# A chunked linear-attention scan with a SoLU feed-forward: units batch by batch, whole-tensor loads, and DMA transposes from unit 12 on

## The chip, the cores and the metric

The kernel runs on one core of one Trainium2 chip. The metric is the device time in microseconds (us) of one execution. The core has TensorE (PE, its weight loads PEld), VectorE (DVE), ScalarE (ACT), GpSimd (POOL) and SyncE (SP). In this kernel SP issues every DMA, and 16 DMA engines move the bytes.

## The reference

Per batch and head a 48 x 48 state is decayed and fed token by token; the output of all heads goes through a feed-forward with SoLU and a norm.

```python
batch, n_heads, seq, head_dim = (4, 8, 768, 48)      # r, k, v, w: float32 of this shape; u: (8, 48)
n_tokens, d_model, d_ff = (3072, 384, 1024)
for t in range(S):
    cur = np.einsum('bhd,bhe->bhde', u[None] * kt, vt)
    y[:, :, t] = np.einsum('bhd,bhde->bhe', rt, state + cur)
    state = wt[:, :, :, None] * state + np.einsum('bhd,bhe->bhde', kt, vt)
...
x = y.transpose(0, 2, 1, 3).reshape(B * S, H * D)
h = x @ w_in
e = np.exp(h - h_max)
sm = e / (np.sum(e, axis=-1, keepdims=True) + 1e-09)
solu = h * sm
ln = (solu - mu) / np.sqrt(var + 1e-06) * g_ln
return (ln @ w_out).astype(np.float32)
```

## The kernel before

The sequence is cut into 6 chunks of 128 tokens. A unit is one chunk of one batch with all 8 heads, so there are 24 units. Before, unit i is chunk i // 4 of batch i % 4: the four batches go side by side, and a unit's state comes from the unit four earlier.

A unit goes through these steps. The names are the words of the order, the engine stands in brackets. LW, LK, LR, LV [SP] load w, k, r, v as float32, 192 KB each, in runs of 48 numbers. lw [ACT] takes the logarithm of w; cum [PE] sums it within the chunk; ex [ACT] takes the exponential; kp [DVE] scales k and r with it. krk and krr [PE] turn the scaled k and r (8 matmuls with an identity) into PSUM and kr [ACT or DVE] copies them out. M [PE] forms the scores, m [ACT or DVE] copies them, masked by sel [POOL] where ACT copied. p, q, qh [POOL] and dg [DVE] form the bonus of u, dv [POOL] multiplies it with v, which vb casts. Y [PE] forms the attention output (with the state if the chunk is not a batch's first), y [ACT or DVE] copies it. S [PE], et [ACT] and st [DVE] update the state. X [PE] turns y with 3 matmuls, and xT copies it.

The feed-forward: H [PE] multiplies with w_in, in 24 matmuls of 128 columns, so that the hidden numbers lie on the partitions and the tokens along the free side. e [ACT] is exp(h), he [DVE] is h times e, ea [POOL] adds halves of e for some units, hq [ACT or DVE] squares he. Oa and Ob [PE] multiply he with the centred, gained w_out (w2, 384 columns and one for the sum), and sum e (or ea) and hq with one-column matmuls into the same bank. sq [ACT], qm [DVE] and lv [ACT] (a logarithm and an exponential) give the norm's scale, o [ACT or DVE] applies it, out [SP] stores 192 KB.

The program is written out in one string, ORDER (lines 21 to 67). Each word names a step, a unit, and where there is a choice an engine or a PSUM bank. The class InOrder ties each instruction to the one before it on its engine, so every engine, SP's DMA issues too, works strictly in the sequence of the string. The weights are loaded, gained (gw), averaged (mn) and centred (ce) in the same string; hot are matmuls on zeros at the start. Nearly every instruction is recorded at line 86, the helper's, so the profile tells groups apart by tiles. Where a ring of buffers is short (NIO = 7 input buffers, NWK = 4, NKP = 6), a load or a write waits for the last reader.

Of the kernel before, what the change touches and what calls it, by code (L numbers as in the profile page):

```python
# [8 lines left out]
F32 = mybir.dt.float32  # L9
# [11 lines left out]
ORDER = """  # L21
LW2 LU0 ik0 lw2 hot5.4 cum2.0 LW1 lw1 us0.7 ih0 LW3 lw3 cum3.2 LR2 uc0 ex2 LK2 p2 LV2 vb2.p kp2 hot4.4 krk2.6 krr2
LR1 LK1 cum1.4 LW0 ex1 kp1 kr2.d hot1.0 S2.7 lw0 et2 LV1 vb1.d LW4 st2 p1 q1 hot2.0 krk1.1 krr1 q2 qh2 dg2 LG0
kr1.a M2.4 ex3 hot1.0 M1.6 m1.d dv2 LR0 LK0 p0 q0 cum0.0 ex0 lw4 cum4.6 ex4 kp0 krk0.1 krr0 LR3 gs0.0 gc0 dg1
m2.d Y2.i0 kr0.d LK3 p3 LR4 LV0 vb0.a dg0 dv1 kp3 Y1.i5 hot3.1 krk3.4 krr3 LK4 kp4 M0.2 m0.d krk4.1 y1.a X1.5
krr4 y2.a X2.0 dv0 xT2.d hot1.6 Y0.n7 y0.d kr3.a M3.2 hot1.0 X0.6 S1.4 p4 q3 kr4.a xT1.a xT0.a LI2 LI1 wi1.a
M4.0 m4.a et1 LI0 S0.5 et0 wi0.d m3.d LO1 wi2.p H1.6 e1 gw5.a H2.0 e2 H0.2 LO0 gw2.a q4 qh4 dg4 qh3 dg3 gw4.p
gw7.p LV3 vb3.p dv3 sel4 LW6 e0 gw6.d st1 LV4 vb4.p he1 lw6 dv4 gw1.d LW5 gw0.d gw3.d mn0.4 mc0 ce5.p ce6.p
Y3.i7 ce4.p he2 st0 he0 cum6.0 y3.a ce7.p hot1.5 X3.6 lw5 xT3.a ce3.d LK6 LR6 p6 Y4.n5 LR5 LK5 ce2.d hq0.a ex6
LW7 cum5.2 H3.6 p5 y4.d ex5 ce1.d ce0.d Oa0.5 kp6 krk6.1 krr6 S4.0 hq1.d Oa1.4 kp5 krk5.3 krr5 X4.2 Ob1 e3 he3  # L30
LV5 q6 q5 kr5.d hq2.a et4 st4 M5.6 kr6.a M6.0 xT4.d lw7 cum7.2 hq3.a sq1 m6.a m5.d dg5 vb5.d qm1 dv5 Ob0 ex7 sq0
qm0 S3.7 qh6 LR7 LK7 p7 kp7 et3 lv1 st3 lv0 H4.0 Y5.n6 y5.d LR9 LK8 o1.d e4 krk7.3 krr7 Oa2.2 he4 X5.7 q7 kr7.d
LW9 lw9 o0.a LK9 p9 LW8 lw8 S5.6 et5 cum9.4 ex9 Ob2 sq2 LR8 p8 st5 dg6 kp9 qm2 LV6 xT5.a LV9 vb6.p dv6 sel6
cum8.0 ex8 kp8 hq4.a LV7 LV11 out1 LW10 dg7 vb7.p dv7 Oa3.3 vb9.a lv2 H5.6 e5 M7.4 m7.d he5 q8 krk9.1 LK10 krr9
kr9.a S9.0 et9 Ob3 sq3 st9 q9 qm3 o2.a out0 ea5.p Y6.i5 y6.a LV8 LR10 Y7.n4 y7.d LW11 LW12 krk8.1 M9.6 lw10 lv3
X6.2 xT6.a m9.d o3.a krr8 LV10 out3 out2 kr8.d qh9 dg9 dg8 hq5.d cum10.4 ex10 kp10 S6.0 vb11.d et6 X7.2 xT7.a
st6 p10 vb8.d dv8 dv9 H6.6 e6 he6 H7.2 lw11 e7 he7 M8.4 m8.a Oa5.1 Y9.n0 Ob5 sq5 y9.d cum11.6 ex11 krk10.5 krr10
qm5 kr10.d S7.4 et7 st7 Oa4.3 hq6.d lv5 lw12 o5.a X9.2 sel8 Y8.i0 vb10.p y8.a LK11 LR11 kp11 xT9.d q10 dg10 p11
M10.4 m10.a sel10 S10.1 et10 st10 dv10 S8.0 et8 S11.7 et11 X8.6 xT8.a LK12 LW13 cum12.4 q11 ex12 lw13 st11 st8
Ob4 sq4 qm4 LW14 LR12 kp12 p12 lw14 lv4 o4.a out5 LK13 LV12 LR13 Y10.n2 dg11 y10.d H8.6 e8 krk12.1 krk11.0 krr11  # L40
krr12 kr12.d he8 kr11.a q12 qh12 cum13.4 H9.2 vb12.p S12.1 ex13 p13 q13 ea7.p dg12 kp13 dv11 LW16 LR14 LK14 e9
he9 et12 st12 M12.6 m12.a Oa6.0 X10.5 xT10.a krk13.4 krr13 kr13.a M11.6 m11.d ea8.p dv12 sel12 p14 cum14.2 ex14
q14 out4 Ob6 sq6 hq8.d M13.4 m13.d LV13 hq7.a LW15 lw15 lw16 kp14 vb13.d H10.6 dg13 qm6 LW18 lw18 Y11.n1 y11.d
Oa8.5 LK16 LR15 LR16 LK15 e10 he10 hq9.a krk14.4 Y12.i3 krr14 lv6 qh14 kr14.d p15 ea10.p dv13 LR18 LV14 vb14.p
q15 qh15 LK18 p18 Ob8 sq8 qm8 y12.a S13.2 et13 st13 o6.a lv8 X11.1 xT11.d cum16.6 ex16 X12.3 hq10.d LW19 kp16
Oa9.4 cum15.0 xT12.a Ob9 ex15 kp15 sq9 o8.a dg14 dv14 qm9 M14.2 m14.a sel14 krk16.7 Oa7.6 krr16 kr16.d lv9 o9.d
cum18.0 ex18 kp18 Ob7 LV15 S14.5 et14 st14 krk15.3 krr15 kr15.d LK19 Y13.i2 lw19 cum19.0 krk18.7 p16 q16 vb15.a
S15.4 y13.a sq7 qm7 dg15 X13.5 xT13.d ex19 LR19 kp19 lv7 o7.a q18 krr18 kr18.d H11.2 et15 st15 krk19.5 krr19
kr19.d LW17 lw17 cum17.0 e11 he11 ex17 ea11.p out8 LK17 LR17 p17 kp17 H12.6 e12 he12 hq11.a p19 H13.4 e13 Oa10.3
Y14.n2 M16.0 m16.a dg16 q19 dv15 y14.d ea12.p ea13.p M15.6 m15.d he13 Ob10 sq10 X14.2 out9 Oa11.1 LW20 qm10 lw20  # L50
cum20.6 hq12.d krk17.0 krr17 out6 out7 LV16 vb16.a dv16 xT14.a S16.2 LR20 ex20 LK20 dg18 et16 st16 lv10 o10.a
H14.4 e14 kp20 Ob11 sq11 kr17.d LK23 qm11 lv11 o11.a Oa12.2 krk20.3 krr20 kr20.a he14 sel16 Y16.n7 y16.d Y15.n6
y15.d M19.4 m19.a M18.0 m18.d Ob12 X15.7 xT15.a q17 hq13.d LV19 LW21 LV17 X16.3 xT16.a ea14.p vb19.a M17.4 m17.d
sq12 LK22 out10 qm12 dg17 qh19 vb17.p sel19 p20 hq14.a LW22 LV20 q20 qh20 dv17 M20.0 LV21 m20.d out11 LK21 H15.6
e15 he15 lw22 ea15.p H16.4 LV18 vb18.p dv18 LR21 p21 lw21 Oa14.3 Y17.n1 LR22 LV23 q21 dg19 dv19 Ob14 LR23 p23
p22 e16 he16 lv12 Oa13.0 LW23 o12.a out12 sq14 qm14 hq15.d vb20.a lv14 dg20 dv20 y17.d cum21.6 ex21 Ob13 cum22.4
sq13 ex22 LV22 vb22.p ea16.p o14.d out14 Y18.n2 y18.d Oa15.1 X18.3 qm13 kp22 lv13 xT18.d X17.2 xT17.a kp21 Ob15
sq15 qm15 S18.5 et18 st18 Y19.n4 y19.d lv15 o15.a out15 o13.a krk22.2 S17.3 et17 lw23 H18.6 e18 ea18.p hq16.d
vb21.d st17 Y20.n5 y20.d X19.4 xT19.d krr22 kr22.a H17.0 he18 hq18.d cum23.4 ex23 kp23 Oa16.3 e17 ea17.p he17
krk21.2 krr21 kr21.a H19.6 e19 krk23.5 X20.4 krr23 q22 qh21 vb23.p out13 xT20.a kr23.a he19 Oa18.2 Ob16 sq16  # L60
M21.0 q23 ea19.p qh23 dg22 dv22 m21.a sel21 qm16 lv16 M22.6 hq19.a M23.4 Ob18 sq18 dg21 H20.0 o16.a out16 m22.d
m23.d Oa19.7 Y22.n6 qm18 lv18 hq17.d Ob19 S19.5 dg23 dv23 e20 Oa17.4 y22.d X22.3 he20 et19 st19 xT22.d dv21
Y21.n6 Ob17 y21.d sq19 o18.a sq17 qm17 lv17 Y23.n1 out18 qm19 lv19 X21.0 xT21.d H22.2 o17.a e22 out17 ea20.p
y23.d H21.0 X23.5 xT23.a e21 hq20.d o19.d out19 Oa20.6 he22 hq22.d H23.4 e23 he21 hq21.d Ob20 sq20 qm20 lv20
o20.a out20 ea22.p Oa22.7 ea21.p Oa21.3 he23 hq23.d Ob22 sq22 qm22 lv22 Ob21 sq21 qm21 lv21 o21.d o22.a out22
out21 ea23.p Oa23.2 Ob23 sq23 qm23 lv23 o23.a out23
"""

NIO, NLW, NKP, NWK = 7, 10, 6, 4
# [24 lines left out]
def kernel(  # L94
# [22 lines left out]
    units = [(c, b) for c in range(NC) for b in range(B)]  # L117
# [30 lines left out]
    w_t = ring("w_in", NIO, [C, H, 64], F32)  # L148
    kr_t = ring("kr_in", NIO, [C, 2, H, 64], F32)
    v_t = ring("v_in", NIO, [C, H, 64], F32)  # L150
    win_f = consts.tile([128, KM, DF], F32)
    wout_f = consts.tile([128, KF, DM], F32)
    o_t = ring("o", NWK, [C, DM], F32)
# [28 lines left out]
    dve.memset(inv_col, 1.0 / RDF)  # L182
    ones_row = consts.tile([1, C], F32)
# [23 lines left out]
    st_t = [ring(f"st{b}_", 2, [C, H, D], BF16) for b in range(B)]  # L207
    xT_t = ring("xT", NWK, [128, KM, C], BF16)
    e_t = ring("e", NWK, [128, KF, C], BF16)
    ea_t = ring("ea", NWK, [128, KF // 2, C], BF16)  # L210
    he_t = ring("he", NWK, [128, KF, C], BF16)
    hq_t = ring("hq", NWK, [128, KF, C], BF16)
    sq_t = ring("sq", NWK, [C, 2], F32)
    qm_t = ring("qm", NWK, [C, 1], F32)
    lv_t = ring("lv", NWK, [C, 1], F32)
# [26 lines left out]
    def rows_of(src, i):  # L242
        c, b = units[i]
        return src[b, :, c * C:(c + 1) * C, :].rearrange("h t d -> t h d")

    def load_w(i, x):
        sp.dma_start(out=w_t[i % NIO][:, :, :D], in_=rows_of(w, i))

    def load_k(i, x):
        sp.dma_start(out=kr_t[i % NIO][:, 0, :, :D], in_=rows_of(k, i))  # L250

    def load_r(i, x):
        sp.dma_start(out=kr_t[i % NIO][:, 1, :, :D], in_=rows_of(r, i))

    def load_v(i, x):
        sp.dma_start(out=v_t[i % NIO][:, :, :D], in_=rows_of(v, i))
# [63 lines left out]
    def log_w(i, x):  # L320
        act.activation(out=lw_t[i % NLW][:, :, :D], in_=w_t[i % NIO][:, :, :D], func=LN)
# [11 lines left out]
    def scaled(i, x):  # L333
        ex = live[i]["ex"][:, :, :DM].rearrange("t a (h d) -> t a h d", h=H)
        dve.tensor_mul(out=kp_t[i % NKP][:, :, :, :D], in0=ex, in1=kr_t[i % NIO][:, :, :, :D])

    def bonus_rk(i, x):
        kr = kr_t[i % NIO]
        pool.tensor_mul(out=p_t[i % 3], in0=kr[:, 0, :, :D], in1=kr[:, 1, :, :D])
# [10 lines left out]
    def v_cast(i, x):  # L350
        copy = {"a": act.copy, "d": dve.tensor_copy, "p": pool.tensor_copy}[x]
        copy(out=vb_t[i % NLW], in_=v_t[i % NIO][:, :, :D])
# [49 lines left out]

    def attend(i, x):
        L = live[i]
        c, b = units[i]
        m, kr, vb = m_t[i % NWK], kr_s[i % NKP], vb_t[i % NLW]
        y_ps = L["y_ps"] = bank([C, DM], F32, x[-1], "y_ps")
        first = True
# [175 lines left out]
```

## Time and profile before

| what | value |
|---|---|
| median of 3 runs | 155.5 us (154.58 to 156.43) |
| span of the profiled execution, first to last instruction | 152.4 us |
| what the median has above that span | 3.1 us |
| mean granted TensorE clock | 0.975 |
| busy: PE, DVE, ACT, POOL | 136.4, 131.8, 120.0, 119.0 us |
| DMA moved | 27.06 MB in 104,825 packets, 100,314 of them under 512 bytes |
| a load of k, r or w: issue to landing | 3.7 us (median) |
| a store of a unit: issue to landing | 2.6 us (median) |

The profile is of one execution and gives it no other time than its span; the runs' times also hold what lies ahead of the first and behind the last instruction. Busy time is the union of a group's instructions; a matmul's end is modelled, so two matmuls in sequence overlap on paper, and their distance from start to start says what they cost. The slices are 40 equal parts of the span, a digit is a tenth of busy time.

### The profile page before, as it was taken

How to read it: one execution, taken by the hardware profiler on the slowest of the kernel's cores; microseconds unless marked ns; L12 is line 12 of the kernel's file. 1: busy time of each engine (PE TensorE's matmuls, PEld its weight loads, DVE VectorE, ACT ScalarE, POOL GpSimd, SP SyncE). 2: the span in 40 equal slices, each digit the busy share in tenths (PEclk: the TensorE clock that was granted, in tenths of full speed). 3: DMA queues.
4: the chain of work that ended last, by engine and by line, in shares of the span. 5: the costliest groups of instructions: out<-in, count | busy, mean ns of one | idle time of the engine just before them, and what ended most of it. 6: DMA issues, size and time to landing. Idle time of an engine off the chain costs nothing.

```text
span 152.4 us, 5172 instructions
## 1 busy us (share of the span) xinstructions
PE 136.4 (90%) x2093; PEld 105.5 (69%) x2093; DVE 131.8 (87%) x227; ACT 120.0 (79%) x247; POOL 119.0 (78%) x149
## 2 busy tenths in 40 slices
PE   6777598968999999999998999999799999999970
PEld 1242365936778889779776689887686988889740
DVE  5029968899999999998999999999999999988940
ACT  4526648869888999799998889998988789938661
POOL 7268986799909994899999997799889979973600
PEclk9959969999999999999999999999999999999998
DMA  3999999989979999989897989995998110112023
GB/s 76 218 216 211 217 334 377 254 175 223 216 151 216 220 204 229 206 177 224 194 203 144 228 195 275 199 199 136 241 205 210 63 45 4 44 63 103 4 79 127
DMA packets 104825, 27.06 MB, mean 178 GB/s; under 512 B 100314, under 2 KB 104419, under 8 KB 104803
## 3 DMA queue, kind: packets, MB, share of 16 engines
q1 hardware_dynamic: 104802, 26.75, 77.4%
q8 instruction: 16, 0.26, 0.7%
q14 instruction: 7, 0.05, 0.1%
HBM read 22.03 MB, written 4.72 MB: 176 GB/s over the span
## 4 chain that ended last, share of the span: by engine, by line
PE 53%; DVE 23%; SPq 8%; ACT 6%; issue 3%; DMA 2%; POOL 1%; DVEq 0%; POOLq 0%
PE ps L86 53%; SPq L86 7%; DVE he L86 6%; DVE m L86 4%; DVE kp L86 4%; DVE w L86 3%; DMA kr_in<-in_k_dram 2%; DVE kr L86 1%; DVE hq L86 1%; DVE y L86 1%; DVE st L86 1%; ACT ps L86 1%; ACT o L86 1%; DVE dg L86 1%; ACT win_sb L86 1%
## 5 line engine op out<-in xcount | busy, mean ns | idle before, releaser
L86 PE MATMUL ps<-w,he 128*128 128x385 bf16 x192 | 44.5, 325 | 1.0 <-DVE w L86 0.7
L86 PE MATMUL ps<-xT,win_sb 128*128 128x128 bf16 x576 | 35.5, 219 | 1.1 <-DVE qm L86 0.8
L86 PEld LDWEIGHTS <-win_sb 128*128 128x128 bf16 x576 | 32.8, 98 | 2.2 <-DVE m L86 0.9
L86 PE MATMUL ps<-one_col,hq 128*128 128x1 bf16 x192 | 31.5, 164 | 0.0
L86 DVE TENSOR_TENSOR he<-ps,e 128x1024 bf16<-128x1024 f32 x24 | 29.1, 1214 | 1.6 <-ACT e L86 1.6
L86 DVE TENSOR_TENSOR kp<-ps,kr_in 128x768 bf16<-128x768 f32 x24 | 22.8, 951 | 7.7 <-DMA kr_in<-in_k_dram 4.9
L86 POOL TENSOR_TENSOR p<-kr_in 128x384 bf16<-128x384 f32 x24 | 24.7, 1038 | 4.5 <-DMA kr_in<-in_k_dram 4.2
L86 POOL TENSOR_TENSOR dv<-vb,dg 128x384 bf16<-128x384 bf16 x24 | 21.7, 907 | 7.5 <-DVE qm L86 3.6
L86 ACT ACTIVATE e<-ps 128x1024 bf16<-128x1024 f32 x24 | 24.5, 1021 | 3.1 <-PE ps L86 2.0
L86 POOL TENSOR_TENSOR ea<-e 128x512 bf16<-128x512 bf16 x17 | 20.0, 1181 | 6.4 <-ACT e L86 5.7
L86 POOL TENSOR_TENSOR q<-p,u_bc 128x384 bf16<-128x384 bf16 x24 | 22.2, 931 | 2.4 <-DVE dg L86 1.7
L86 ACT ACTIVATE ps<-ps 128x768 f32<-128x768 f32 x24 | 19.1, 799 | 5.1 <-PE ps L86 4.3
L86 PEld LDWEIGHTS <-kp 128*128 128x128 bf16 x272 | 17.5, 100 | 6.0 <-DVE kp L86 3.2
L86 PEld LDWEIGHTS <-he 128*128 128x128 bf16 x192 | 18.4, 96 | 4.0
L86 PEld LDWEIGHTS <-hq 128*128 128x128 bf16 x192 | 15.4, 96 | 8.3
L86 DVE TENSOR_TENSOR m<-ps,keep 128x1024 bf16<-128x1024 f32 x15 | 18.2, 1216 | 1.2 <-PE ps L86 1.0
L86 PE MATMUL ps<-ident,kp 128*128 128x128 bf16 x192 | 16.5, 227 | 1.6 <-POOL p L86 1.1
L86 DVE TENSOR_TENSOR hq<-he 128x1024 bf16<-128x1024 bf16 x15 | 13.4, 890 | 0.1
L86 ACT COPY kr<-ps 128x1024 bf16<-128x1024 bf16 x11 | 11.1, 1012 | 2.4 <-PE ps L86 2.4
L86 ACT ACTIVATE lw<-w_in 128x384 bf16<-128x384 f32 x23 | 11.7, 523 | 1.3 <-DMA w_in<-in_w_dram 1.3
L86 PEld LDWEIGHTS <-kr 64*128 64x128 bf16 (+1 forms) x272 | 10.2, 95 | 3.1 <-ACT kr L86 0.7
L86 PE MATMUL ps<-inv_col,ea 128*128 128x1 bf16 x68 | 11.2, 165 | 0.0
(90 smaller groups left out, 293.7 us busy)
## 6 DMA issues: line engine op xcount, KB each, us to landing
w_in<-in_w_dram SPq DMA_DIRECT2D x24, 192.0 KB, 3.7
kr_in<-in_r_dram SPq DMA_DIRECT2D x24, 192.0 KB, 3.7
kr_in<-in_k_dram SPq DMA_DIRECT2D x24, 192.0 KB, 3.7
v_in<-in_v_dram SPq DMA_DIRECT2D x24, 192.0 KB, 3.6
out_dram<-o SPq DMA_DIRECT2D x24, 192.0 KB, 2.6
win_f<-in_moe_w_in_dram SPq DMA_DIRECT2D x3, 512.0 KB, 6.4
wout_f<-in_moe_w_out_dram SPq DMA_DIRECT2D x2, 768.0 KB, 9.0
u_row<-in_u_dram SPq DMA_DIRECT2D x1, 1.5 KB
```

The source lines that it names most:

```text
L86: made = make(*args, **kwargs)
```

## The change

- Unit i is now chunk i % 6 of batch i // 6: one batch after the other. The state of a unit comes from the unit just before it, and one ring of three state tiles serves all.
- The inputs live in two tiles, each for a whole batch and all four tensors. Batches 0 and 1 are still loaded unit by unit; batches 2 and 3 by one transfer per tensor (BW, BK, BR, BV; 1,152 KB each), which overwrite batches 0 and 1. w_out is staged in the tile of batch 1, and w_in shares a tile with the output buffers and with the rows of he.
- For units 12 to 23 the turn of k and r (kt) and of y (xt) is a DMA transpose issued by SP; the 8 and 3 matmuls on PE and the copies out of PSUM go.
- For units 12 to 22 hidden is formed by rows, the tokens on the partitions, in 6 matmuls of 512 columns. The exponential and the square on ACT add up along the row as they go, so the one-column matmuls for e and hq go. he is written by rows and turned by a DMA transpose (ht, 256 KB).
- The norm's scale is formed on DVE (sums) and on GpSimd: a subtraction and a power of minus one half, in place of two squares, a logarithm and an exponential on ACT.
- ORDER is written anew. The weights stand near its start, the whole-tensor loads between unit 5 and unit 16, ea is left for 4 units.

The DMA part of the new order, SP's queue from the first whole-tensor load on (other engines' words left out):

```text
BW2 out4 LW9 LK9 LR9 out3 LV9 BK2 out5 LW10 LK10 LR10 LV10 BR2 LW11 LK11 LR11 LV11 kt12 BV2 kt13 kt14 BW3 out6
kt15 xt12 BK3 kt16 xt13 BR3 ht12 out8 out7 kt17 xt14 kt18 BV3 ht13 out9 kt20 xt15 kt19 xt16 out11 xt17 out10 ht14
kt21 xt18 kt22 ht15 xt19 out12 ht17 kt23 xt21 ht16 out13 xt20 ht18 xt22 ht19 xt23 out14 out15 ht21 ht20 out17 ht22
out16 out19 out18 out21 out20 out23 out22
```

```diff
-NIO, NLW, NKP, NWK = 7, 10, 6, 4
+NLW, NKP, NWK, NHQ, NEA, NHT = 7, 6, 4, 4, 4, 3
...
-    units = [(c, b) for c in range(NC) for b in range(B)]
+    units = [(b, c) for b in range(B) for c in range(NC)]
...
-    w_t = ring("w_in", NIO, [C, H, 64], F32)
-    kr_t = ring("kr_in", NIO, [C, 2, H, 64], F32)
-    v_t = ring("v_in", NIO, [C, H, 64], F32)
-    win_f = consts.tile([128, KM, DF], F32)
-    wout_f = consts.tile([128, KF, DM], F32)
-    o_t = ring("o", NWK, [C, DM], F32)
+    in_t = ring("in", 2, [C, 4, H, NC, D], F32)
+    staged = in_t[1].rearrange("p s h c d -> p (s h c d)")
+    wout_f = staged[:, 4 * H * NC * D - KF * DM:].rearrange("p (a n) -> p a n", a=KF)
+    late = consts.tile([128, KM * DF], F32, name="late")
+    win_f = late.rearrange("p (a n) -> p a n", a=KM)
+    o_t = [late[:, j * DM:(j + 1) * DM] for j in range(NWK)]
+    ht_t = [late[:, NWK * DM + j * DF // 2:NWK * DM + (j + 1) * DF // 2].bitcast(BF16) for j in range(NHT)]
...
+    minus_half = consts.tile([C, 1], F32)
+    dve.memset(minus_half, -0.5)
...
-    st_t = [ring(f"st{b}_", 2, [C, H, D], BF16) for b in range(B)]
+    st_t = ring("st", 3, [C, H, D], BF16)
...
+    k_in, r_in, w_in, v_in = 0, 1, 2, 3
+
+    def chunk(kind, i):
+        b, c = units[i]
+        return in_t[b % 2][:, kind, :, c, :]
...
+    def load(src, kind, i):
+        b, c = units[i]
+        sp.dma_start(out=chunk(kind, i), in_=src[b, :, c * C:(c + 1) * C, :].rearrange("h t d -> t h d"))
+
+    def load_all(src, kind, b):
+        sp.dma_start(out=in_t[b % 2][:, kind], in_=src[b].rearrange("h (c t) d -> t h c d", t=C))
...
+    def turned_kr(i, x):
+        sp.dma_start_transpose(out=kr_s[i % NKP], in_=kp_t[i % NKP].rearrange("t a h d -> t (a h d)"))
+
+    def turned_x(i, x):
+        sp.dma_start_transpose(out=xT_t[i % NWK], in_=y_t[i % NWK])
...
     def hidden(i, x):
         xT = xT_t[i % NWK]
+        if i in by_rows:
+            h_ps = live[i]["h_ps"] = bank([C, 2, 512], F32, x, "h_ps")
+            for j in range(KM):
+                for n in range(2):
+                    pe.matmul(h_ps[:, n, :], lhsT=xT[:, j, :], rhs=win_sb[:, j, n * 512:(n + 1) * 512],
+                              start=(j == 0), stop=(j == KM - 1))
+            return
...
     def hidden_exp(i, x):
+        if i in by_rows:
+            act.activation(out=e_t[i % NWK].rearrange("p a t -> p (a t)"), in_=live[i]["h_ps"].rearrange("p a n -> p (a n)"),
+                           func=EXP, accum_out=be_t[i % NWK])
+            return
...
+    by_rows = {int(word[2:].split(".")[0]) for word in ORDER.split() if word.startswith("ht")}
...
     def hidden_mul(i, x):
+        if i in by_rows:
+            dve.tensor_mul(out=ht_t[i % NHT], in0=live[i]["h_ps"].rearrange("p a n -> p (a n)"),
+                           in1=e_t[i % NWK].rearrange("p a t -> p (a t)"))
+            return
...
+    def turned_he(i, x):
+        sp.dma_start_transpose(out=he_t[i % NWK], in_=ht_t[i % NHT])
+
     def hidden_square(i, x):
-        he, hq = he_t[i % NWK], hq_t[i % NWK]
+        if i in by_rows:
+            act.activation(out=hq_t[i % NHQ].rearrange("p a t -> p (a t)"), in_=ht_t[i % NHT], func=SQUARE, accum_out=s2_t[i % NWK])
+            return
+        he, hq = he_t[i % NWK], hq_t[i % NHQ]
...
-            pe.matmul(o_ps[:, :DM + 1], lhsT=he[:, f, :], rhs=w2[:, f, :], start=(f == 0), stop=False,
+            pe.matmul(o_ps[:, :DM + 1], lhsT=he[:, f, :], rhs=w2[:, f, :], start=(f == 0), stop=(f == KF - 1 and i in by_rows),
                       skip_group_check=True)
+            if i in by_rows:
+                continue
...
     def sums(i, x):
-        act.activation(out=sq_t[i % NWK], in_=live[i]["o_ps"][:, DM:DM + 2], func=SQUARE)
-
-    def variance(i, x):
-        dve.tensor_sub(out=qm_t[i % NWK], in0=live[i]["o_ps"][:, DM + 2:], in1=sq_t[i % NWK][:, 0:1])
+        o_ps = live[i]["o_ps"]
+        square = s2_t[i % NWK] if i in by_rows else o_ps[:, DM + 2:]
+        dve.tensor_scalar(out=var_t[i % NWK], in0=o_ps[:, DM:DM + 1], scalar1=o_ps[:, DM:DM + 1], scalar2=square,
+                          op0=MULT, op1=SUB)
+        if i not in by_rows:
+            total = o_ps[:, DM + 1:DM + 2]
+            dve.tensor_scalar(out=eps_t[i % NWK], in0=total, scalar1=total, scalar2=1e-6 * DF * DF, op0=MULT, op1=MULT)
+
+    def spread(i, x):
+        be = be_t[i % NWK]
+        pool.tensor_scalar(out=eps_t[i % NWK], in0=be, scalar1=be, scalar2=1e-6 * DF, op0=MULT, op1=MULT)
 
     def scale(i, x):
-        act.activation(out=lv_t[i % NWK], in_=sq_t[i % NWK][:, 1:2], func=LN, scale=1e-6 * DF * DF,
-                       bias=qm_t[i % NWK])
-        act.activation(out=rs_t[i % NWK], in_=lv_t[i % NWK], func=EXP, scale=-0.5)
+        rs = rs_t[i % NWK]
+        pool.tensor_tensor(out=rs, in0=eps_t[i % NWK], in1=var_t[i % NWK], op=SUB)
+        pool.tensor_tensor(out=rs, in0=rs, in1=minus_half, op=ALU.pow)
```

## The prediction

> **What bounds the kernel now.** I read the engine totals and slices first, then the chain that ended last, then single spacings on PE, then what SP and the DMA engines do.
>
> ```profile
> span 152.4 us, 5172 instructions
> ...
> PE 136.4 (90%) x2093; PEld 105.5 (69%) x2093; DVE 131.8 (87%) x227; ACT 120.0 (79%) x247; POOL 119.0 (78%) x149
> ...
> PE   6777598968999999999998999999799999999970
> ...
> DMA  3999999989979999989897989995998110112023
> GB/s 76 218 216 211 217 334 377 254 175 223 216 151 216 220 204 229 206 177 224 194 203 144 228 195 275 199 199 136 241 205 210 63 45 4 44 63 103 4 79 127
> ...
> q1 hardware_dynamic: 104802, 26.75, 77.4%
> ```
>
> Two resources are full. The DMA engines are at nine tenths from the second slice to about 115 us, then nearly idle. PE is at nine tenths from 43 us on. The window 43 to 73 us has PE busy 29.94 of 30.0 us and a DMA share of 0.96. So the loads set the pace of the first two thirds about as much as PE, and the DMA engines have a free last quarter that the change wants to use. The chain of waits over the end shows that PE alone ends the run:
>
> ```profile
> 110.34 37.23 PE ps L86 x601
> ...
> 147.60 0.18 ACT sq L86
> ...
> 147.80 0.17 DVE qm L86
> ...
> 148.00 0.30 ACT lv L86
> ...
> 148.32 0.21 ACT rs L86
> ...
> 148.56 0.58 ACT o L86
> ```
>
> One piece of 601 matmuls runs without a gap up to 147.6 us; the last unit's scale, output copy and store take 4.8 us behind it. What a matmul costs there is its distance to the next start, not its modelled length. The timeline of PE:
>
> ```profile
> 112.29 0.32 PE L86 MATMUL ps<-w,he 128*128 128x385 bf16 x1
> 112.45 0.17 PE L86 MATMUL ps<-one_col,hq 128*128 128x1 bf16 x1
> 112.48 0.33 PE L86 MATMUL ps<-st,kr 128*128 128x96 bf16 x4
> ...
> 119.83 1.50 PE L86 MATMUL ps<-xT,win_sb 128*128 128x128 bf16 x24
> 121.17 0.33 PE L86 MATMUL ps<-st,kr 128*128 128x96 bf16 x4
> ...
> 124.56 0.61 PE L86 MATMUL ps<-ident,kp 128*128 128x128 bf16 x8
> 125.01 1.50 PE L86 MATMUL ps<-xT,win_sb 128*128 128x128 bf16 x24
> ```
>
> An output matmul takes 0.16 us, a one-column one 0.025, hidden's 24 take 1.34, a turn of k and r 0.45 (8 matmuls), a turn of y 0.17. Summed over the program these spacings give 124 us before, 113.5 after.
>
> **The change part by part.** *PE loses* 12 x (0.45 + 0.17) = 7.4 us of turns, 88 one-column matmuls of hq (11 units, 2.2 us), and 124 - 88 = 36 of e and ea (0.9 us): 10.5 us. Hidden by rows is six 512-column matmuls for 24 short ones: by the 385-column spacing 0.16 x 512/385 x 6 = 1.3 us against 1.34, so nothing. If PE stays the only bound, the span is 152.4 - 10.5 = 141.9 us.
>
> *The other engines.* DVE loses 9 kr copies (682 ns), 11 hq (890), 4 xT (349), 3 vb (635), 2 m (1216) and 24 qm (151) and gains 37 small statistics (about 150), 3 o (610) and a little of the weights: 131.8 to about 115 us. ACT loses sq, lv and rs (24 x 0.67 = 16 us), 3 kr and 8 xT, gains 11 hq (1055) and 2 m: about 114 us. POOL loses 13 ea (1181) and 5 qh (548), gains 3 vb, 2 masks and per unit a subtraction and a power on one column. No row shows a power. Bounds: 98 ns (its smallest memset) and 548 ns (192 columns) each, so 4.8 to 26 us for 48 of them and POOL between 109 and 130 us. I take the low side, since one column is nearest to the memset. At the end of a unit the old chain sq to rs takes 0.9 us; the new one takes two DVE (0.30) and two POOL instructions, 0.5 to 1.4 us. No gain is counted. Were the cover gone, the upper end costs 0.5 us in the tail.
>
> *Transposes on the DMA engines.* 35 are added: 23 of 256 KB (k with r, 12; he, 11) and 12 of y with 96 KB, 7.2 MB. No row has one. The cheapest row per byte is a weight load (377 GB/s in the slice): 19 us. The load rows move 192-byte pieces at 216 GB/s: 33 us. If read and write of SBUF each cost a load's time: 66 us. A bf16 row of 128 elements is a piece of 256 bytes, nearest to the load, so 33 us. [...]
>
> *First half.* Batch by batch means that unit 12 cannot start before whole tensors of batch 2 have landed. Ahead of BR2's end SP's order has 62 unit-tensors (12.2 MB at 216 GB/s: 56.4 us), the weights (3.15 MB at about 355: 8.9) and 6 stores (1.18 MB; the window 130 to 140 us holds stores alone, share 0.18 at 68 GB/s, which is 2.65 us per MB: 3.1). Together 68.4, at the share of 0.96 71.3, plus 1.8 for the start and 2 to land: 75. SP also waits for the centred w_out before LW6, since batch 1 lies where w_out was, and for o0 to o5 ahead of loads; 1 us for both, so kp12 and the first transpose come at 76 us. By the spacings 47 us of PE's work stand before kt12 in the order, and H6 behind it needs nothing from it. That is what a PE that is full from 43 us (19 us done there) has done by 74, so it loses little.
>
> *Second half.* After H6 65 us of PE's work are left. In the window 76 to 147 us PE was busy 69.45 of 71.0, so 66.5 us, plus the tail 4.8: **76 + 66.5 + 4.8 = 147.3 us**. The DMA engines must in the same time bring LV11, BV2 and batch 3 (6.1 MB, 28 us), 18 stores (9.4) and the transposes (33): 70.4 us, ending at 146.4. They are as full as PE. The 10.5 us of PE are therefore about half lost: the gain is 5.1 us of span. Where the stall goes: kp18 waits for BR3, whose queue position is behind kt16 and xt13, and the in-order DVE keeps y, he and m of other units behind kp18.
>
> The profiled execution has a span of 152.4 us; the median of the runs is 155.5, 3.1 more. With 3.1 on top the forecast is **150.4 us**.
>
> **The rivals.**
> 1. *PE alone counts.* The transposes cost the 19 us of the cheap row, the DMA engines keep ahead, nothing gates kp12: 141.9 + 3.1 = 145.0 us. For it: the DMA slices from 115 us on are nearly empty. Against it: kp12's loads still need 75 us.
> 2. *SP's queue becomes the bound (slower).* SP issues in order, one thing at a time; the timeline of its queue shows what an issue takes.
>
> ```profile
> 44.68 3.51 SPq L86 DMA_DIRECT2D v_in<-in_v_dram  x4
> 48.28 0.65 SPq L86 DMA_DIRECT2D out_dram<-o  x1
> 48.98 0.42 SPq L86 DMA_DIRECT2D w_in<-in_w_dram  x1
> ```
>
> A free issue is 0.42 us, a held one 0.9, the longest load issue 2.1. From xt17 on the order leaves 25 us of PE's work for 19 transposes (12 large, 7 of y) and 6 stores; with the stores at 0.42 it decides from (25 - 2.5)/19 = 1.18 us per transpose. At 2.1 the queue needs 42.4 us and the span grows by 17.4; midway between 1.18 and 2.1, 1.64, by 8.7: 147.3 + 8.7 + 3.1 = **159.1 us**. For it: every he, kr and xT of the last ten units passes this one queue, between stores that wait for o. Against: a free issue of 1024 pieces is only 0.42. [...]
> 3. *Transposes held behind whole-tensor loads.* BV2 to BV3 each fill the engines for 1.18 MB/216 GB/s = 5.5 us, and a transpose issued behind one waits for it. If two of the five catch a turn that PE has no other work for, 5.5 us net: 155.9, no change. For it: one queue. Against it: H6 to H11 stand free to fill.
> 4. *A transpose moves smaller pieces than I take*, 66 us instead of 33: the DMA sum ends 33 us later, with a third of it covered by PE's idle tail and the stores: 172.
>
> **How the numbers follow.** Forecast 0.37, rival 1 0.17, rival 2 0.27, rival 3 0.09, rival 4 0.10. The predicted time is that of the forecast. The range begins at 142.5 (rival 1 with 2.5 us less at the start, since the weights are moved up in SP's order) and ends at 166, which takes in rival 2 up to 2.0 us per transpose and leaves out its end and rival 4. The likeliest case alone has 146 to 154. A measurement of this kernel can tell about 1% (1.6 us) from no change. Faster by more: forecast and rival 1, less the forecast's upper edge, 0.52. Within 1%: rival 3 and that edge, 0.11. Slower: rivals 2 and 4, 0.37.
>
> **What would show it.** Right: a q1 share near 95%, DMA slices full nearly to the end, first transpose at 74 to 78 us, PE's total near 125, issues of transposes under 1.1 us. Rival 1 shows as PE gapless from 45 us. Rival 2 shows as long SP pieces in the chain and PE waiting for DMA of kr, xT or he late; rival 3 as the same waits only behind whole-tensor loads. The forecast is wrong if kp12 comes before 70 or after 82 us, or if a transpose takes the engines more than 1.5 us.

## The result, and the profile after

The changed kernel takes **180.7 us** (median of four runs, 179.8 to 181.4) where the kernel before takes 155.0: a ratio of 1.164, interval 1.156 to 1.171. The forecast was 150.4 us with a range to 166. All five cases of the prediction lie below the measured time. The medians and ratios here and below leave out executions that took over 1.5% more than the fastest of the same kernel.

The page of the kernel after:

```profile
span 179.7 us, 4277 instructions
...
PE 139.4 (78%) x1632; PEld 92.8 (52%) x1641; DVE 121.0 (67%) x211; ACT 116.3 (65%) x199; POOL 121.0 (67%) x193
...
PE   7847787798979674969929892958959798789890
...
PEclk9997899999999655599996998586996999999999
DMA  5999999899996899969999969698778477665864
...
q1 hardware_dynamic: 96578, 33.96, 84.6%
...
DMA 26%; PE 18%; SPq 15%; DVE 13%; POOL 9%; ACT 8%; issue 8%; POOLq 0%; DVEq 0%; ACTq 0%
```

The change did what it says: 461 matmuls are gone and the DMA engines work to the end. But PE, at nine tenths before in all but two slices from 43 us to the tail, is now below that in 26 of the 40 slices, no compute engine is over 78%, and the last line, the shares of the chain that ended last, is led by DMA and has a seventh in SP's queue. Engine time of a queue is its share times the span: 0.846 x 179.7 = 152.0 us for q1, where before had 0.774 x 152.4 = 118.0.

The windows of 20 us of the kernel after (PE, PEld, DVE, ACT, POOL busy, then the granted clock, the DMA share and GB/s):

```profile
60.00:80.00 20.00, 14.45 (x156) 10.11 (x157) 12.91 (x20) 11.48 (x22) 11.52 (x14) 0.58 0.87 196
80.00:100.00 20.00, 16.48 (x254) 13.99 (x254) 15.12 (x22) 13.48 (x21) 15.36 (x22) 0.91 0.98 187
100.00:120.00 20.00, 15.29 (x193) 10.13 (x191) 11.75 (x21) 13.15 (x23) 13.12 (x18) 0.83 0.85 168
120.00:140.00 20.00, 15.71 (x151) 9.22 (x154) 14.34 (x24) 11.40 (x22) 15.35 (x24) 0.83 0.82 181
140.00:160.00 20.00, 16.50 (x169) 8.86 (x169) 15.87 (x25) 14.16 (x29) 13.82 (x23) 1.00 0.68 155
```

Of these windows only the one from 80 to 100 us has the DMA engines really full; after that neither they nor PE are. Work waits in turn, first for one and then for the other. The timeline of SP's queue shows how:

```profile
80.88 1.68 SPq L79 DMA_TRANSPOSE kr<-kp  x1
83.17 0.73 SPq L79 DMA_DIRECT2D in<-in_v_dram  x1
84.02 8.63 SPq L79 DMA_TRANSPOSE kr<-kp  x2
93.12 0.70 SPq L79 DMA_DIRECT2D in<-in_w_dram  x1
...
103.14 0.73 SPq L79 DMA_DIRECT2D in<-in_k_dram  x1
103.96 6.97 SPq L79 DMA_TRANSPOSE kr<-kp  x1
...
112.69 0.70 SPq L79 DMA_DIRECT2D in<-in_r_dram  x1
113.49 6.10 SPq L79 DMA_TRANSPOSE he<-late  x1
...
125.17 0.72 SPq L79 DMA_DIRECT2D in<-in_v_dram  x1
127.78 5.52 SPq L79 DMA_TRANSPOSE he<-late  x1
...
136.61 1.30 SPq L79 DMA_TRANSPOSE kr<-kp  x1
138.00 1.21 SPq L79 DMA_TRANSPOSE xT<-y  x1
```

A whole-tensor load is issued in 0.7 us. Behind four of the five loads shown the next transpose is held: 8.6 us for two, 7.0, 6.1, 5.5. The next load stands behind the held transpose in the same in-order queue. So BV2, BW3, BK3, BR3 and BV3 go out at 83, 93, 103, 113 and 125 us: 42 us from the first to the last. A free transpose takes 1.2 to 1.3 us of SP, for the 96 KB of y as for 256 KB. The hold is not special to transposes: earlier, behind BK2 a store took 5.9 us of SP (at 61.15 us) and behind BR2 the unit load LW11 6.8 us (at 71.07).

The chain of waits shows who pays:

```profile
83.17 9.28 DMA in<-in_v_dram
...
99.38 3.93 DMA kr<-kp
...
112.69 7.98 DMA in<-in_r_dram
...
152.89 4.72 DMA kr<-kp
...
159.80 2.71 DMA he<-late
...
166.19 2.72 DMA he<-late
```

V of batch 2 and r of batch 3 are late from the loads; later it is turned data that lands late. The list of waits adds up, over the whole run, what the in-order engines lost to such transfers (total, times, longest):

```profile
POOL p L79 <- DMA in<-in_r_dram: 15.5, 9, 4.3
...
ACT lw L79 <- DMA in<-in_w_dram: 10.7, 4, 5.9
...
PEld L79 <- DMA kr<-kp: 7.8, 6, 3.5
```

Of p's 15.5 us 4.9 fall ahead of 58 us, 6.3 between 58 and 80 and 5.9 after (a wait across a border counts in both); of lw's 10.7 us 5.9 lie between 58 and 80 and none after. So part of this was lost behind BK2 and BR2, before the first transpose.

### The profile page after: what moved, and what is told of

Same layout as the page of the kernel before. It is cut to its first block, busy times and chain, and to the rows that moved or that the text cites. A ratio compares the mean times of both kernels' runs of the same rounds, so it can differ in the third digit from the quotient of the medians.

```text
span 179.7 us, 4277 instructions
## 1 busy us (share of the span) xinstructions
PE 139.4 (78%) x1632; PEld 92.8 (52%) x1641; DVE 121.0 (67%) x211; ACT 116.3 (65%) x199; POOL 121.0 (67%) x193
## 4 chain that ended last, share of the span: by engine, by line
DMA 26%; PE 18%; SPq 15%; DVE 13%; POOL 9%; ACT 8%; issue 8%; POOLq 0%; DVEq 0%; ACTq 0%
PE ps L79 18%; SPq L79 14%; DMA in<-in_r_dram 8%; DMA in<-in_v_dram 5%; DMA kr<-kp 5%; DMA in<-in_moe_w_out_dram 4%; DMA he<-late 3%; POOL rs L79 3%; DVE kp L79 3%; POOL p L79 2%; DVE late L79 2%; ACT ps L79 2%; DVE he L79 2%; POOL q L79 2%; ACT e L79 2%
## 5 line engine op out<-in xcount | busy, mean ns | idle before, releaser
L79 POOL TENSOR_TENSOR p<-in 128x384 bf16<-128x384 f32 x24 | 23.9, 999 | 15.5 <-DMA in<-in_r_dram 15.5
L79 DVE TENSOR_TENSOR kp<-ps,in 128x768 bf16<-128x768 f32 x24 | 22.5, 953 | 15.3 <-ACT ps L79 10.8
L79 POOL TENSOR_TENSOR q<-p,u_bc 128x384 bf16<-128x384 bf16 x24 | 21.8, 914 | 1.3 <-ACT u_bc L79 0.6
L79 PE MATMUL ps<-xT,win_sb 128*128 128x128 bf16 x312 | 21.0, 228 | 0.0
L79 PEld LDWEIGHTS <-win_sb 128*128 128x128 bf16 x312 | 19.7, 103 | 1.7 <-issue 0.5
L79 PEld LDWEIGHTS <-kp 128*128 128x128 bf16 x176 | 12.5, 106 | 15.3 <-issue 9.2
L79 ACT ACTIVATE lw<-in 128x384 bf16<-128x384 f32 x23 | 11.5, 523 | 10.7 <-DMA in<-in_w_dram 10.7
L79 PE MATMUL ps<-win_sb,xT 128*128 128x512 bf16 x59 | 16.2, 392 | 2.1 <-DVE st L79 1.3
L79 PE MATMUL ps<-one_col,hq 128*128 128x1 bf16 x104 | 17.1, 165 | 0.3
L79 DVE TENSOR_TENSOR he<-ps,e 128x1024 bf16<-128x1024 f32 x13 | 15.8, 1221 | 1.1 <-ACT e L79 1.0
L79 DVE TENSOR_TENSOR st<-ps,et 128x384 bf16<-128x384 f32 x20 | 11.0, 550 | 7.8 <-ACT et L79 7.8
L79 ACT CAST m<-ps 128x1024 bf16<-128x1024 f32 x11 | 11.1, 1010 | 7.1 <-PE ps L79 6.9
```

The costliest lines, as they stand in the source:

```text
L79: made = make(*args, **kwargs)
```

## The experiments

The kernel before took 154.4 to 155.1 us beside each of them. Three places in SP's order serve as milestones: the first transpose (kt12), xt15 (the fourteenth of the 35 transposes) and the last he.

### Which resource: loads, transposes or queue

**E1, unit loads.** Each whole-tensor load is split into the six unit loads of its batch, in its place.

```diff
-... e5 BW2 out4 ...
+... e5 LW14 LW12 LW13 LW15 LW16 LW17 out4 ...
```

> The changed kernel with each whole-tensor load of batches 2 and 3 replaced, in the same place of SP's order, by six loads of one unit each (in the order in which they are used); the bytes, and everything else, stay. Theory A (SP and the one DMA queue are the bound: what follows a whole-tensor load on SP is held 5.5 to 8 us, because its pieces stand ahead in the queue, whatever the size of the transfers): same bytes in the same places, so 176 to 184 us. Theory B (it is the whole-tensor form: unit 12 waits for six units' worth of each tensor, and one issue holds SP): 160 to 168 us. Theory C (the batch-by-batch order itself, one chain of states): no change, 178 to 183 us.

Measured: 175.7 us, ratio 1.139 (1.118 to 1.160). No transpose is held over 2.4 us any more, but the same waits are there, in small pieces: SP is busy 18.8 to 19.3 us of every 20 from 80 to 160 us, and six unit loads take 4.7 to 6.6 us of it. The split gives back 5 of the 26 us, so the size of a load is a small part of the loss.

**E6, whole-tensor loads on another queue.**

```diff
-        sp.dma_start(out=in_t[b % 2][:, kind], in_=...)
+        act.dma_start(out=in_t[b % 2][:, kind], in_=...)
```

> The changed kernel with its eight whole-tensor loads issued by ScalarE in place of SP, at the same words of the order, so that they go through another queue; transposes, unit loads and stores stay on SP. Theory A (what stands behind a whole-tensor load in the one queue is held until its pieces have gone: transposes and stores 5.2 to 8.6 us each on SP): SP's long pieces vanish, 166 to 173 us. Theory D (the 16 DMA engines are simply full): no change, 178 to 183 us. If ScalarE is held in its turn by the issues: above 181 us.

Measured: 182.4 and 186.2 us; the trace is of the second, so only the mechanism is read from it. The timelines of its SP and ACT queues (the first two lines are SP's, the third is ACT's):

```profile
86.51 9.03 SPq L79 DMA_TRANSPOSE kr<-kp  x3
...
104.55 5.53 SPq L79 DMA_TRANSPOSE kr<-kp  x1
...
115.90 4.11 ACTq L79 DMA_DIRECT2D in<-in_r_dram  x1
```

Transposes are held although the load is in another queue, and so is a load behind a load in ACT's. BV2 went out on ACT's queue at 87.1 us and BW3 at 100.5. So the hold doesn't need one queue shared with the load; what makes it the traces don't show. And ACT's order brings the loads no earlier than SP's did: there BW3 went out at 93.1 us.

**E2 and E3, the turns back on PE** (E3 with E1's unit loads as well). Krk, krr, X and the copies return for units 12 on, and H, he and ea go by columns.

```diff
-... q11 kt12 lw11 ...
+... q11 krk12.1 krr12 kr12.a lw11 ...
```

> The changed kernel with all 35 DMA transposes taken back: k, r and y of units 12 to 23 are turned by TensorE and copied out by VectorE or ScalarE at the same places of the order, and hidden of units 12 to 22 is formed as in units 0 to 11. Whole-tensor loads, unit order and the power on GpSimd stay. Theory A (transposes share SP's queue with whole-tensor loads and wait 5.5 to 8 us behind them, and from 133 us on SP issues transposes back to back at 1.25 us): 156 to 163 us. Theory B (whole-tensor loads gate by themselves): 168 to 176 us. Theory C (the order by batches leaves PE idle, clock at half): 172 to 180 us.

> Both edits at once: no DMA transposes and no whole-tensor loads; the unit order, the order of the words and the power on GpSimd stay. Theory A: 154 to 160 us, hardly below the kernel without transposes alone. Theory B: 154 to 160 us, and clearly (8 us or more) below the kernel without transposes alone. Theory C: 170 us or more, since the batch-by-batch order is still there.

Measured: 185.9 (1.205) and 186.5 us (1.209), above all that was expected. In both the DMA engines are nearly idle from 120 to 160 us (share 0.09, then 0.06), yet PE is busy only 16.6 and 16.3 of 20 us there, and POOL's rs waits 32.4 us in all for DVE's eps in E2. The order was laid out without these copies; an explanation that was not tried is that, put where the transposes stood, they stall the in-order engines. These two runs don't price a transpose.

**E5, plain copies.** The 35 transposes become copies of the same bytes that don't turn.

```diff
-        sp.dma_start_transpose(out=kr_s[i % NKP], in_=kp_t...)
+        sp.dma_start(out=kr_s[i % NKP].rearrange("p a t -> p (a t)"), in_=kp_t...)
```

> The changed kernel with each of the 35 DMA transposes replaced by a plain DMA copy of the same bytes between the same tiles: the turning is left out, so k, r, y and he reach TensorE unturned. The places in SP's queue and every wait stay; what falls is the price of a transpose itself (issue 1.25 us against about 0.43, pieces of 256 bytes at 21.8 ns against rows of 768 and 2048 bytes). If the transposes' own price decides: 160 to 167 us. If what decides is that they stand in one queue behind whole-tensor loads and wait for their producers: 173 to 179 us.

Measured: 165.8 us (1.075; 1.053 to 1.096). q1 falls to 0.814 x 163.1 = 132.8 us, 19 less, and an issue on SP from 1.2 to between 0.47 and 0.6 us.

**E9, E11, E10: loads left out.** E9 leaves out the four loads of batch 3, E11 all eight whole-tensor loads (the later units work on old data), E10 is E11 with E5's plain copies.

```diff
-... ex16 BW3 y12.a ...
+... ex16 y12.a ...
```

> The changed kernel without the four whole-tensor loads of batch 3 (4.7 MB, about 21 us of all 16 DMA engines): units 18 to 23 read what batch 1 left in the tile. Theory D (the DMA engines are full from 80 to 135 us, and the queue only shows it): 158 to 167 us. Theory E (the transposes' own latency, issue 1.25 us and 2.4 to 3.6 us to land, on an in-order PE): 173 to 179 us. Theory C (the order by batches): 176 to 181 us.

> The changed kernel without all eight whole-tensor loads (9.4 MB, 42 us of the DMA engines): batches 2 and 3 read what batches 0 and 1 left. Theory D: the run is 25 us or more faster, 148 to 156 us, and the first transpose comes before 72 us in place of 80.9. Theory E: 165 to 174 us, transposes still waited for. Theory C: 172 us or more.

> As the one without whole-tensor loads, and the transposes replaced by plain copies too (the turning is left out): what is left is the order itself with its engines. PE's sum by spacings is 113.5 us against 124.4 before. If DMA was all of the loss: 140 to 147 us. If the order by batches, or GpSimd's scale ahead of each output, holds the engines: 155 us or more.

Measured: 167.4 (1.083; 1.077 to 1.089), 157.3 (1.017; 1.011 to 1.023) and 155.3 us (1.004; 1.000 to 1.009). Without the loads beside them, the 35 transposes cost 1.9 us over plain copies; with them, 14.9. Without the transposes' price the loads cost 10.5 (E5 against E10), with it 23.4. So the two meet: 13 us belong to neither alone.

**E16, E17, E18: engine time or SP's time?** E5 took both away. E16 gives the DMA engines their load back (k, r and he copied in pieces of 256 bytes), E17 gives SP's back (one load of 256 bytes after each copy), E18 both.

```diff
# E16
-    kr_s = ring("kr", NKP, [C, 2 * HP, C], BF16)
+    kr_s = [t[:, :, :C] for t in ring("kr", NKP, [C, 2 * HP, C + 4], BF16)]
# E17, after each copy
+        sp.dma_start(out=next(spare), in_=u.rearrange("(o h) d -> o (h d)", o=1)[:, :64])
```

> The changed kernel with its 35 transposes replaced by plain copies of the same bytes that do not turn (so k, r, y and he of units 12 on reach PE unturned), as in the run that took 165.8 us, but k with r and he go in pieces of 256 bytes, as the transposes do, where that run's copies had larger ones. It gives the copies back the engine time of the transposes (some 15 us more than the large pieces, q1 near 150 us of 16 engines' time) at the short issue of 0.5 to 0.6 us on SP. Theory A, the DMA engines' fill sets the loss: 176 to 181 us. Theory B, SP's queue sets it, where a transpose's issue takes 1.2 to 1.3 us: 164 to 168 us. A value between shares it out.

> The changed kernel with plain copies for the transposes (165.8 us; unturned data as there), and after each copy one load of 256 bytes into a tile of its own that nothing reads. It takes SP's time (0.4 to 0.6 us each, so that copy and load together take about the 1.2 us of a transpose) and hardly any of the DMA engines'. Theory A (the engines' fill): 165 to 169 us. Theory B (SP's queue): 176 to 181 us.

> Both edits at once: copies in pieces of 256 bytes and a small load behind each, so that the engines and SP are loaded as by the transposes (unturned data as there). If engine time and issue time are all that a transpose costs, it comes back to 177 to 184 us. If it stays under 174 us, a transpose costs something that neither a copy of its pieces nor SP's time shows, such as its landing.

Measured: 165.2 (1.069; 1.060 to 1.079), 170.1 (1.098; 1.091 to 1.106) and 169.7 us (1.098; 1.094 to 1.102). The q1 lines of E16 (its trace is of a run of 170.7 us, span 168.9) and E18:

```profile
q1 hardware_dynamic: 92946, 33.96, 86.0%
```

```profile
q1 hardware_dynamic: 93016, 33.97, 86.9%
```

That is 145 us of engine time in both, 12.5 more than E5, and it costs nothing that can be told (E16 against E5, E18 against E17). The longer occupation of SP costs 4 us. So the engine time that copies in small pieces take isn't the loss, and SP's time is a part of it. E18 ends 11 us below the changed kernel, and under the 174 us of its expectation: a transpose costs more than these two. Its copy with the small load takes 0.60 + 0.51 = 1.11 us of SP where a large transpose takes 1.25 to 1.3, and its DMA engines carry 6.6 us less than the changed kernel's. Landing doesn't tell the two apart: E16's copies land in 3.9, 3.0 and 3.2 us (kr, he, xT; medians), the transposes in 3.6, 2.8 and 2.4.

The holds behind whole-tensor loads are there with copies too. E18's SP queue behind BV2, BK3 and BR3:

```profile
80.55 5.08 SPq L79 DMA_DIRECT2D kr<-kp  x1
...
97.99 5.39 SPq L79 DMA_DIRECT2D kr<-kp  x1
...
106.14 5.25 SPq L79 DMA_DIRECT2D he<-late  x1
```

With the one behind BV3 the four add up to 20.2 us in E18 and 19.3 in E5, against 27.2 in the changed kernel, and from BV2 to BV3 go by 37.0, 34.5 and 42.0 us. Less the free issue of each held transfer (0.60, 0.47 and 1.27 us) these are 17.8, 17.0 and 20.9 us. So a hold isn't made by turning, and where the held transfers turn the four are 3 to 4 us longer in sum. What of the 11 us is due to turning itself stays open.

The milestones, in us from the start:

| kernel | kt12 | xt15 | last he | kt12 to xt15 | xt15 to last he |
|---|---|---|---|---|---|
| after | 80.9 | 135.4 | 169.5 | 54.5 | 34.1 |
| E18 | 78.0 | 126.2 | 156.1 | 48.2 | 29.9 |
| E5, plain copies | 77.9 | 122.4 | 152.0 | 44.5 | 29.6 |
| E9, no batch 3 | 79.9 | 120.8 | 155.2 | 40.9 | 34.4 |
| E11, no whole loads | 73.6 | 111.0 | 145.0 | 37.4 | 34.0 |
| E10, E11 with copies (a run of 156.2 us) | 74.3 | 111.5 | 143.4 | 37.2 | 31.9 |

From xt15 on the three kernels with transposes need the same 34 us, with or without loads. The loss is in the stretch ahead of it, where the loads go out: 17 us between E11 and after, and 7 more before kt12. Ahead of kt12 E5, E9 and E18 do the same work as the changed kernel and yet reach it between 77.9 and 79.9 us, not at 80.9; so up to 3 us of such a difference owe nothing to the transposes.

### GpSimd's power, and the floor

**E4, the kernel before with the power alone.** Sums, variance and scale as in the change; all else stays.

```diff
-        act.activation(out=lv_t[i % NWK], in_=sq_t[i % NWK][:, 1:2], func=LN, ...)
-        act.activation(out=rs_t[i % NWK], in_=lv_t[i % NWK], func=EXP, scale=-0.5)
+        pool.tensor_tensor(out=rs, in0=eps_t[i % NWK], in1=var_t[i % NWK], op=SUB)
+        pool.tensor_tensor(out=rs, in0=rs, in1=minus_half, op=ALU.pow)
```

> The kernel before with the norm's scale alone changed: sums on VectorE, subtraction and power on GpSimd. PE bounds it from 43 us on, and the last unit's chain grows from 0.9 to about 1.2 us: 0 to 1 us slower than before, 154.5 to 156 us. If GpSimd, then near 130 us busy, holds dv and p: 157 to 160 us.

Measured: 185.2 us (1.200; 1.193 to 1.207), 30 us more than before. Its list of waits:

```profile
ACT o L86 <- POOL rs L86: 43.5, 14, 8.7
...
POOL rs L86 <- DVE eps L86: 13.8, 7, 3.7
...
PE ps L86 <- ACT o L86: 9.2, 5, 6.3
```

The scale is cheap by itself (0.21 and 0.57 us a unit on POOL); but POOL reaches it in its own order, behind p, q, dv and ea of other units. ACT stands in front of o until then, up to 8.7 us at a time, and PE waits 9.2 us in all for o, which frees its bank.

**E15, E4 without the 17 ea** that POOL adds.

```diff
-... out0 ea5.p Y6.i5 ...
+... out0 Y6.i5 ...
```

> The kernel before with the scale's subtraction and power on GpSimd, as in the run that took 185.2 us, and without the 17 ea products on GpSimd (the part of the output that they make is left out; hq of those units then sums the old content of the ea buffers). That takes 17 x 1.18 = 20 us off GpSimd, as much as the new order takes off it (13 ea and 5 qh, 18 us). Theory: the 30 us of that run were GpSimd's load in the old order, with o on ScalarE and PE's banks waiting behind long ea and vb instructions on the in-order engine; without the ea the time falls to 156 to 166 us. Rival: the wait itself costs it, since ScalarE's o now waits for a unit's whole chain through GpSimd wherever o stands in the order; then 175 us or more remain.

Measured: 170.9 us (1.104; 1.094 to 1.115). Other than the expectation says, nothing is left out: for a unit without ea PE sums all of e, four one-column matmuls more each. Taking 20 us off POOL gives 14 of the 30 back; 16 remain, and in the trace (of a run of 174.1 us) ACT's o still waits 27.1 us for POOL's rs. So both theories are half right: the load and the place in the order.

**E7, the changed kernel with the scale on ACT; E14, with E1's unit loads too; E13, E11 with the scale on ACT.**

```diff
-        pool.tensor_tensor(out=rs, in0=eps_t[i % NWK], in1=var_t[i % NWK], op=SUB)
-        pool.tensor_tensor(out=rs, in0=rs, in1=minus_half, op=ALU.pow)
+        act.activation(out=rs, in_=var_t[i % NWK], func=LN, scale=-1.0, bias=eps_t[i % NWK])
+        act.activation(out=rs, in_=rs, func=EXP, scale=-0.5)
```

> The changed kernel with the norm's subtraction and power taken from GpSimd (0.19 and 0.55 us a unit) and given back to ScalarE as a logarithm and an exponential (about 0.5 us a unit); everything else stays. If GpSimd's backlog behind the late r (120.8 to 131 us in the chain) decides: 174 to 178 us. If the power lies off the path: 179 to 182 us.

> The changed kernel with both mends at once: each whole-tensor load split into six unit loads in its place, and the scale on ScalarE. The two alone gave 175.7 and 177.8 us, against 180.7. If the DMA engines' fill is what is left and the two mends act on different waits, their gains add: 171 to 174 us. Rival: both gains are the same wait seen twice (GpSimd starts p behind the landing of r), and together they give no more than the larger one: 175 to 177 us.

> The changed kernel without its eight whole-tensor loads (the units of batches 2 and 3 then work on what batches 0 and 1 left in the buffer, so part of the computation is fed with other data) and with the scale's logarithm and exponential on ScalarE instead of the subtraction and power on GpSimd; the 35 transposes stay. Without the loads alone the kernel took 157.3 us, where PE's work by its spacings would end at 141.9 + 3.1 = 145. Theory: the remaining 12 us are GpSimd, which was busy 19.2 and 19.5 us of each 20 us between 80 and 120 us; taking 24 x 0.74 us = 18 us off it, about 9 of them in the second half, brings the time to 148 to 152 us. Rival: the order and the landing of the transposes set the floor; then 155 to 158 us.

Measured: 177.8 (1.150; 1.143 to 1.157), 179.0 (1.157; 1.148 to 1.166) and 157.8 us (1.020; 1.013 to 1.027). E7 is 3 us below the changed kernel, but E14 is 3 us above E1, and E13 is no faster than E11. So in the new order the power on POOL costs about 3 us at most, and the gains of E1 and E7 don't add; E14 missed both of its ranges. My theory of E13 fell: with 17 us taken off POOL the kernel without loads stays where it was. Its windows:

```profile
80.00:100.00 20.00, 19.34 (x311) 14.57 (x310) 18.76 (x33) 18.66 (x38) 18.18 (x24) 1.00 0.36 65
100.00:120.00 20.00, 18.94 (x209) 11.26 (x211) 17.93 (x30) 19.17 (x43) 16.31 (x22) 1.00 0.72 139
120.00:140.00 20.00, 17.22 (x170) 9.57 (x172) 14.64 (x25) 15.59 (x37) 9.00 (x16) 1.00 0.75 158
```

From 80 to 120 us DVE and ACT are at 92 to 95% beside PE's 96%, and then all of them thin out. So even without the loads two elementwise engines are nearly as full as PE in this stretch, which speaks against 145 us, PE alone, in this order. What exactly holds the last 10 us was not tried.

### Transposes in the idle quarter of the kernel before

**E8** gives kt21 to kt23 and xt18 to xt23 to the DMA engines in the kernel before, in its own order, where the engines are idle. **E12** does it for kt21, kt22, xt19 and xt20 alone, those whose users come latest.

```diff
-... kp21 Ob15 ... krk21.2 krr21 kr21.a H19.6 ...
+... kp21 kt21 Ob15 ... H19.6 ...
```

> The kernel before with the DMA transposes alone, and only where its DMA engines are idle, after 115 us: k and r of units 21 to 23 and y of units 18 to 23 are turned by DMA; nothing else of the change. PE loses 3 x 0.45 + 6 x 0.17 = 2.4 us of turns, and 9 copies go from VectorE and ScalarE. If a transpose costs its 1.25 us of SP and 2.4 to 3.6 us to land, in slack: 1 to 2.4 us faster than before, 152 to 153.5 us. If the landing lies on the chain of the last units (turn to hidden), or SP waits for an output ahead of it: 1 to 4 us slower.

> The kernel before with DMA transposes only where their result has 5 us or more to land in the trace of before: k and r of units 21 and 22, y of units 19 and 20. PE loses 2 x 0.45 + 2 x 0.17 = 1.2 us, VectorE and ScalarE four copies. If only exposed landings made the nine turns slower than the kernel before: 0.5 to 1.2 us faster than before. If SP's queue with its stores does: equal or up to 1 us slower.

Measured: 157.4 (1.016; 1.011 to 1.022) and 154.5 us (0.998; 0.995 to 1.001). The chain of E8:

```profile
116.23 4.30 DMA xT<-y
...
127.57 3.89 DMA kr<-kp
...
141.13 2.36 DMA xT<-y
```

PE saves 0.45 or 0.17 us per turn (the spacings in before, at 124.56 and 121.55 us), and the three turns above put 2.4 to 4.3 us of transfer each into the chain that ended last. E12, whose four turns had 5 us or more to land in the trace of before, shows no loss, but no gain can be told either. No version that was run beats the kernel before.

## Why the prediction was wrong, point by point

- **PE's saving** happened (2093 to 1632 matmuls) but was worth nothing: PE is not the bound after. Its busy total rose to 139.4 us, where the prediction looked for 125, at a lower granted clock (0.895).
- **First half.** Kt12 was forecast for 76 us and came at 80.9, inside the 70 to 82 that the text allowed. Not all of its sum fits: 18 of its 62 unit-tensors are the loads BW2, BK2 and BR2, 16 us of the 56.4, and without them E11 reaches kt12 only 7 us earlier, at 73.6; the other work came almost as late, as the text said of PE (74). The rest, some 28 us of the 32 by which the span misses the forecast 147.3, comes after it.
- **Second half, the step that failed.** It set 66.5 us of PE's work beside 70.4 us of DMA and let both run at full rate. The sum of the DMA work was about right: the shares of the windows from 80 us on add up to 79 us, the transposes at 38.4 instead of 33 (28,160 packets of 256 bytes at 21.8 ns over 16 engines, added up from the trace). The list of loads was three short: LW11, LK11 and LR11 stand behind BR2 and are in neither half, 2.7 us at its 216 GB/s. But the two did not run side by side. A load waits in SP's queue behind a held transpose, the transpose behind the load before it, PE and POOL for what lands late. The five loads BV2 to BV3 were priced at 5.5 us of engine time each and took 42 us from the first to the last issue. E9 and E11 give 13 and 23 us back by taking loads away, E5 15 by plain copies, and E16 keeps these 15 although the DMA engines have most of their load back. So what the sum had left out is not more engine time but the price of loads and transposes that hold each other up: 13 us that neither costs alone. Of the transposes' 15 us beside loads 4 are SP's longer issue (E17); the cause of the other 11 stays open.
- **Rival 3** named the mechanism, a transpose held behind a whole-tensor load, and its place. Its price, 5.5 us for two catches, was too low. There were four, 27 us of SP's time, and each also delayed the next load, which was not in the sum at all. E1 shows that smaller loads spread the holds and E6 that another queue doesn't remove them; E5 and E18 show that copies are held as well, so the holds alone don't make up the loss.
- **Rival 2** had the issue right to a tenth: it decides from 1.18 us, measured are 1.2 to 1.3. By itself it costs 1.9 us at most (E11 against E10); beside loads SP's time is worth 4 (E17). The signs that it named are there in part: SP's queue has 15% of the chain, and PE's weight loads wait 7.8 us for kr. Its price, 1.64 us midway to 2.1, was too high: a free large transpose takes 1.25 to 1.3, one of y 1.20. And 2.1 us isn't the longest issue of a load in the kernel before, which has one of 4.11 (v at 24.99 us).
- **Rival 4** is out: 38 us, not 66. 7.2 MB in 38.4 us are 188 GB/s. E5's plain copies took 19 us less for the same bytes, so by an estimate from the two q1 lines about 19, or some 375 GB/s: the cheap row of the weight loads (377 GB/s) fits copies that don't turn, not transposes. E16's in 256-byte pieces took 12.5 us more than E5's.
- **GpSimd** was taken at the low side, about 0.1 us each. The power came out at the upper bound, the subtraction between the two:

```profile
L79 POOL TENSOR_TENSOR rs<-eps,var x24: 186/191/641, 33.8 to 175.5; 128x1 f32<-128x1 f32 x24
L79 POOL TENSOR_TENSOR rs<-rs,minus_half x24: 550/551/568, 34.1 to 175.8; 128x1 f32<-128x1 f32 x24
```

  (shortest, median and longest in ns). It costs 3 us at most here; in the old order it would have been the larger mistake (E4).
- **The floor.** Without any whole-tensor load and with cheap turns the new order takes what the kernel before takes (E10, 155.3). The 10.5 us of PE are lost there too. DVE and ACT, at 92 and 95% of the window from 80 to 120 us in E13, are the likeliest reason, which was not tried; their totals were in the prediction but not set against the window in which they fall.

## What to carry to other kernels

Two resources that are each 95% full by their sums did not run side by side here, where in-order queues tie them together. Price the waits that one causes the other, not only the larger of the two sums, and look at what is issued right behind a long transfer. A transfer that replaced a short PE operation brought 2.4 to 4.3 us of landing into the chain (E8); with 5 us or more to land it cost nothing that can be told (E12, a ratio of 0.998). Moving a tiny operation to another in-order engine cost its place in that engine's order and the load that it added, not only its duration: 0.74 us of GpSimd work per unit cost 30 us in one order and 3 at most in another.

## What the hardware showed that was not expected

- Behind a whole-tensor load of 1.18 MB SP's next issue took 5 to 7 us where it followed at once, whether it was a store, a unit load, a copy or a transpose; with the load in ACT's queue SP's transposes were held too (E6, 9.0 us for three and 5.5 for one). The four kinds of whole-tensor load need 8.1 to 9.4 us from issue to landing (the size printed is that of one piece):

```profile
kr<-kp SPq DMA_TRANSPOSE x12, 3.6
xT<-y SPq DMA_TRANSPOSE x12, 2.4
he<-late SPq DMA_TRANSPOSE x11, 2.8
in<-in_w_dram SPq DMA_DIRECT2D x2, 0.2 KB, 9.4
in<-in_k_dram SPq DMA_DIRECT2D x2, 0.2 KB, 8.1
```

- A power on one column takes 0.55 us of GpSimd, as much as a 192-column product (548 ns), a subtraction 0.19.
- The granted clock fell to 0.58 between 60 and 80 us of the changed kernel (0.50 from 60 to 77 us), where PE was busy 14.45 of 20 us, and its mean was 0.895 against 0.975 before. The kernel without loads had gaps as wide from 60 to 74 us (10.05 of 14 busy) at a granted clock of 1.00. What sets it was not tried, nor what it cost. An estimate, which takes it that PE's time goes with the clock: PE has 32.5 us of the chain that ended last (18.1%), 13 of them in microseconds at 0.50, so 6 to 7 us would go at full clock. In E11 the clock was 1.00 in every window of 20 us from 20 to 140. So the clock is a rival for a few of the lost us that no run here tells apart from the waits.
